# Linear attention and a low-rank mixer on one core: attention of the last batch four slots sooner, one more block pair by half products, second addends added by DMA

## The chip, the core and the metric

The kernel runs on one core of a Trainium2 chip. A core has five engines with their own instruction queues, each worked in program order: TensorE (PE, matrix products into PSUM, with its weight loads shown as PEld), VectorE (DVE), ScalarE (ACT), GpSimd (POOL) and SyncE (SP, here a queue that only issues DMAs). The metric is the device time of one execution in microseconds, as the median of several runs; lower is better.

## The reference

Eight batches, eight heads, 576 positions, head dimension 64. The first part is a linear attention whose features are a rectified input times a cosine and a sine of the position; the second is a low-rank mixing over positions followed by a two-layer network over channels with a residual:

```python
q_p = phi(q); k_p = phi(k)                      # relu(x)*cos, relu(x)*sin -> 128 features
kv  = einsum('bhsf,bhsd->bhfd', k_p, v)
x   = einsum('bhsf,bhfd->bhsd', q_p, kv) / (einsum('bhsf,bhf->bhs', q_p, sum_s k_p) + 1e-6)
x   = heads side by side                        # (8, 576, 512)
u   = x + (x^T @ U @ V)^T                       # rank 32, over positions
out = u + relu(u @ w_ch1) @ w_ch2               # 512 -> 2048 -> 512
```

All inputs and the output are fp32; the kernel computes its products in bf16 with fp32 sums.

## The kernel before

**Tiling.** A batch has 576 positions: four blocks of 128 (the "main" part) and 64 more. The 64 of two batches share one tile of 128, the "tail" of a batch pair. A batch's hidden layer is 2048 wide, 16 blocks of 128, each a unit `g1(b, j)`: four products of 128x128 weights with 512 columns of the transposed input `uT`, and one ScalarE eviction with the maximum into `hid`.

**Half products.** Where it pays in columns, the kernel uses a scheme with seven products in place of eight (sums and differences of quarter matrices, as Winograd's form of Strassen). For the second layer, `half_part(b, n, k, form)` computes output blocks n and n+2 of a batch together by seven steps of eight matmuls with 256 columns; `ORDER["with g"]` is the order of the products, (1, 2, 6, 5, 7, 3, 4). Their addends end in output tiles `o` (block n) and `o2` (block n+2) of the pool tag `o_sb`, a ring of eight buffers: products 1, 6 give first addends of `o`, products 2 and 3 the second ones; 5 and 4 first addends of `o2`, 7 a second one. For batches in `LENT = (5, 6)` the first addends are plain copies by ScalarE, and the input `u` is added by an accumulating DMA from GpSimd in `half_store`, before the block is stored. The sums of `hid` that the scheme needs are `hid_sum` (four for each half of a batch, on VectorE).

For the first layer, `g1_cross(b, p, i)` and `g1_join` do hidden blocks p and p+8 of a batch together ("pair p") by seven products of two matmuls with 256 columns: X and Y in one PSUM bank, Z in another (`CROSS`). ScalarE copies X or Z aside (P1, U2, P5), VectorE adds (C11, C22, C12), ScalarE and VectorE take the maximum. The helpers `opened` (products 1, 2), `sixth`, `fifth`, `third` (product 7) and `closed` (products 3, 4) put these in order. This needs sums of weights, `w1_sum(i, half)` (half 0 serves pairs 0 to 3, half 1 pairs 4 to 7), and of the transposed input, `uT_sum`. The weight sums lie in the buffers in which batch 7's queries and keys were loaded. Batch 7 has all its eight pairs done so, batch 6 its pairs 4 to 7.

**Order.** The order of the work is written out by hand. `slots` is a list of steps on TensorE; `todo` gives for a slot index the work beside it, issued right after the slot's own. From slot 88 the second layer of one batch alternates with the first layer of the next: slots 188 to 219 hold batch 6's first layer (`units`, odd slots from 191) beside batch 5's second (`beside_g`, even slots from 190); from slot 220 batch 7's first layer runs beside batch 6's second, and at the end batch 7's second layer runs alone.

`attention_plan(b)` places a batch's attention relative to a slot `w`, the first number of `PLAN[b]`: for batch 7, query features from w-24 (`q_prep`), key features and value casts from w-14 (`k_prep`, `v_prep`), three DMA transposes of the query features on SyncE (`qtr_dma`) at w-12, w-10, w-8, the two key-value products (`kv_unit`) at w and w+2, five `x_unit` from w+3 in steps of two, the rank-32 product (`A_unit`) at w+14, its expansion (`u_mm`) at w+16 and w+19 with four VectorE adds (`u_add`), two DMA transposes to `uT` (`utr_dma`) at w+17 and w+21, and the tail's part (`u_tail`) at w+23 and w+25. The `x_unit`s share one pair of banks (tag X). Batch 7's inputs are loaded by the plan of batch 6, at slots 149 and 153; batch 6's own `uT` transposes stand at slots 174 and 178.

Of the kernel before, what the change touches and what calls it, by code (L numbers as in the profile page):

```python
# [13 lines left out]
ALU = mybir.AluOpType  # L14
# [3 lines left out]
def kernel(  # L18
# [11 lines left out]
    nc = tc.nc  # L30

    B = 8
# [94 lines left out]
    def cast(eng, o, i):  # L127
        if eng is nc.scalar:
            nc.scalar.activation(out=o, in_=i, func=AF.Copy, bias=0.0, scale=1.0)  # L129
        else:  # L130
            eng.tensor_copy(out=o, in_=i)  # L131


    V_, A_, G_ = nc.vector, nc.scalar, nc.gpsimd
# [34 lines left out]
    def load_v0():  # L169
# [13 lines left out]
        out=iota[:, 0:4], pattern=[[2, 4]], base=0, channel_multiplier=9,  # L183
        allow_small_or_imprecise_dtypes=True,
    )
    for lo in (0, TS):
        nc.gpsimd.iota(
            out=iota[lo : lo + TS, 4:5], pattern=[[1, 1]], base=8, channel_multiplier=18,
# [380 lines left out]
    def g1_main(b, j, half=False):  # L569
        if b not in hid:  # L570
            hid[b] = pool.tile([P, NJ, 512], BF16, tag="hid", bufs=2, name="hid")
        g_ps = g_open.pop((b, j), None)
        d0 = 0 if g_ps is None else 2
        if g_ps is None:
            g_ps = ps.tile([P, 512], FP32, tag="g", bufs=3, name="g_ps")
        if half:
            g_open[b, j] = g_ps
        for d in range(d0, 2 if half else 4):
            nc.tensor.matmul(  # L579
                out=g_ps.rearrange("p (c t) -> p c t", c=4),  # L580
                lhsT=w1_bf[:, d, j * P : j * P + P],
                rhs=uT[b][:, d, :, :],
                start=(d == 0),
                stop=(d == 3),
            )
        if half:
            return
        nc.scalar.activation(  # L588
            out=hid[b][:, j, :], in_=g_ps, func=AF.Relu, bias=0.0, scale=1.0
        )  # L590
# [55 lines left out]
        }[i]()  # L646
        diff(uT_s[b, i], x, y)

    CROSS = [("g0", "g1"), ("g2", "T")]

    def g1_cross(b, p, i):

        if (b, p) not in cross:
            if b not in hid:
                hid[b] = pool.tile([P, NJ, 512], BF16, tag="hid", bufs=2, name="hid")
            of_x, of_z = CROSS[p % 2] if b == B - 1 else (("g0", "g1")[p % 2], "T")
            xy = psum.tile([P, 512], FP32, tag=of_x, bufs=1, name="c_ps")
            cross[b, p] = {"X": xy[:, 0:256], "Y": xy[:, 256:512], "of_z": of_z}  # L660
        w = cross[b, p]
        if i == 5:
            z = psum.tile([P, 512], FP32, tag=w["of_z"], bufs=1, name="c_ps")
            w["Z"] = z[:, 0:256]
        cs = slice(p * P, p * P + P)
        to, lhs, rhs, first = {
            1: lambda: ("X", W1[0], uT_quarter(b, 0, 0), True),
            2: lambda: ("Y", W1[1], uT_quarter(b, 1, 0), False),
            3: lambda: ("Z", w1_s[4], uT_quarter(b, 1, 1), False),
            4: lambda: ("X", W1[3], uT_s[b, 4], False),  # L670
            5: lambda: ("Z", w1_s[1], uT_s[b, 1], True),
            6: lambda: ("X", w1_s[2], uT_s[b, 2], False),
            7: lambda: ("X", w1_s[3], uT_s[b, 3], False),
        }[i]()
        for d in range(2):
            nc.tensor.matmul(  # L676
                out=w[to].rearrange("p (c t) -> p c t", c=2), lhsT=lhs[:, d, cs],
                rhs=rhs[:, d], start=(first and d == 0), stop=(d == 1),
                skip_group_check=not first,
            )  # L680
# [164 lines left out]
    def by_n(t):  # L845
        return t.rearrange("p (j n) -> p j n", n=P)
# [17 lines left out]
    def half_part(b, n, k, form):  # L864


        c2 = n + 2
        i = ORDER[form][k]
        if k == 0:
            halves[b, n] = {  # L870
                "o": [
                    pool.tile([P, DM], FP32, tag="o_sb", bufs=8, name="o_sb") for _ in range(2)
                ]
            }
            if form == "alone":
                halves[b, n]["s"] = pool.tile([P, DM], FP32, tag="o_sb", bufs=8, name="s_sb")
        w = halves[b, n]
        s1, s2 = hid_s.get((b, n, 1)), hid_s.get((b, n, 2))
        to, lhs, rhs = {
            1: ("X", h_of(b, 0, n), W2[0]),  # L880
            2: ("Y", h_of(b, 1, n), W2[2]),
            3: ("Z", h_of(b, 1, n), W2[3]),
            4: ("X" if form == "with g" else "Q", h_of(b, 1, c2), w2_s[3]),
            5: ("Z", s1, w2_s[0]),
            6: ("X", s2, w2_s[1]),
            7: ("X", h_of(b, 0, c2), w2_s[2]),
        }[i]
        at = BANKS[form].get(i)
        if at is not None:
            w[to] = bank(at)  # L890
        acc = w[to][:, 0:256]
        for j in range(8):
            nc.tensor.matmul(  # L893
                out=acc, lhsT=lhs[:, j, :], rhs=rhs[:, j, :],
                start=(j == 0 and at is not None), stop=(j == 7),
                skip_group_check=at is None,
            )
        lo, hi = slice(0, 256), slice(256, 512)
        o, o2 = w["o"]
        u = [[u_of(b, c, g) for g in range(2)] for c in (n, c2)]  # L900

        def first(t, cs, c, g):
            add(V_, by_n(t[:, cs]), u[c][g], by_n(acc))

        def more(t, cs):
            add(V_, t[:, cs], t[:, cs], acc)

        if form == "alone":
            ss = w["s"]
            if i == 1:  # L910
                cast(A_, ss[:, lo], acc)
            elif i == 2:
                first(o, lo, 0, 0)
            elif i == 5:
                cast(A_, o2[:, hi], acc)
            elif i == 6:
                cast(A_, ss[:, hi], acc)
            elif i == 4:
                cast(A_, o2[:, lo], acc)
                add(G_, by_n(o2), by_n(o2), u_bf[b][:, :, c2, :])  # L920
            elif i == 3:
                first(o, hi, 0, 1)
                add(G_, o, o, ss)
            elif i == 7:
                o2v = o2.rearrange("p (g n) -> p g n", g=2)
                add(V_, o2v, o2v, acc.unsqueeze(1).to_broadcast([P, 2, 256]))
        elif i in (1, 6, 5, 4):
            t, cs, c, g = {1: (o, lo, 0, 0), 6: (o, hi, 0, 1), 5: (o2, hi, 1, 1), 4: (o2, lo, 1, 0)}[i]
            if b in LENT:
                cast(A_, t[:, cs], acc)  # L930
            else:
                first(t, cs, c, g)
        elif i == 2:
            more(o, lo)
        elif i == 3:
            more(o, hi)
        else:
            if form == "last":
                more(o2, lo)
            more(o2, hi)  # L940
        if i == 2:
            behind.append(lambda: hid_sum(b, n, 4))
        if k == 6:
            turn[0] += 1

    def half_store(b, n, i):
        eng = nc.gpsimd if b < B - 2 else nc.sync
        c = n + 2 * i
        if b in LENT:
            o = halves[b, n]["o"][i]  # L950
            nc.gpsimd.dma_start(out=by_n(o), in_=u_bf[b][:, :, c, :], accum_op=ALU.add)  # L951
        eng.dma_start(  # L952
            out=out[b].rearrange("(m k) n -> m k n", k=9)[:, c : c + 6 : 5, :],
            in_=halves[b, n]["o"][i],
        )
# [28 lines left out]
    def spare(at):  # L984
# [11 lines left out]
        4: (100, (-20, 1, V_, V_), (-13, 2, A_, V_), -12, (-9, -4, -4)),  # L996
        5: (127, (-24, 2, A_, A_), (-14, 2, A_, V_), (-14, -8, -5), (-8, -4, -4)),
        6: (157, (-23, 2, A_, A_), (-14, 2, A_, V_), (-14, -8, -6), (-8, -4, -4)),
        7: (189, (-24, 2, A_, A_), (-14, 2, A_, V_), (-12, -10, -8), ()),
    }  # L1000

    def attention_plan(b):
# [351 lines left out]
    def g1(b, j):  # L1354
        return lambda: g1_main(b, j)
# [41 lines left out]
    def opened(b, p):  # L1397
        g1_cross(b, p, 1)
        g1_cross(b, p, 2)
        g1_join(b, p, "P1")  # L1400
        g1_join(b, p, "C11")
# [20 lines left out]
    def crossed(*steps):  # L1422
        def go():
            for f, b, p in steps:
                f(b, p)

        return go
# [11 lines left out]
    sums(b6 - 1, 0, (at, at + 1, at + 3))  # L1439
    sums(b6 - 1, 1, (at + 14, at + 16, at + 19))  # L1440
    for i, half, sl in (
        (1, 1, -8), (2, 1, -6), (3, 1, -4), (1, 0, -3), (4, 1, -2), (3, 0, -1), (2, 0, 11), (4, 0, 23),
    ):
        put(at + sl, lambda i=i, half=half: w1_sum(i, half))
    for i in range(4):
        put(at + (1, 2, 3, 7)[i], lambda i=i: uT_sum(b6, i + 1))
    units = [g1(b6, j) for p in range(3) for j in (p, p + 8)] + [g1(b6, 3)]
    units.append(lambda: [opened(b6, 4), g1_main(b6, 11)])
    units.append(crossed((sixth, b6, 4)))
    for p in range(5, 8):  # L1450
        units.append(crossed((opened, b6, p), (fifth, b6, p - 1), (third, b6, p - 1)))
        units.append(crossed((closed, b6, p - 1), (sixth, b6, p)))
    units.append(crossed((fifth, b6, 7), (third, b6, 7)))
# [129 lines left out]
```

## Time and profile before

| | |
|---|---|
| time, median of 3 runs | 292.39 us (292.39 to 292.65) |
| the profiled execution | 293.94 us, its span 292.2 us |
| instructions in the span | 7317 |
| TensorE busy | 283.5 us (97%) |
| VectorE busy | 208.0 us (71%) |
| ScalarE busy | 169.6 us (58%) |
| GpSimd busy | 56.1 us (19%) |
| bytes moved by DMA | 56.19 MB |

A row of a timeline gives the start in us from the span's start, the length, the engine, the line of the kernel, the operation, "written<-read" tiles, the shape, a count where like neighbours are merged and, in brackets, the idle time before it with what ended it. Matmuls are pipelined, so their lengths overlap; what TensorE takes is read from start to start. "SPq" rows are SyncE issuing a DMA, not the transfer. A row of grouped instructions has after the first bar the busy time and the mean length of one in ns, after the second the idle time before and what ended it.

### The profile page before, as it was taken

The numbers are of one execution on the slowest core, as the hardware profiler recorded it, in microseconds if no ns is written. First come the engines' busy times: TensorE is split into PE (matmuls) and PEld (weight loads), VectorE is DVE, ScalarE is ACT, GpSimd is POOL, SyncE is SP. The second block draws the span as 40 slices with busy tenths as digits, with TensorE's granted clock in tenths as the row PEclk, the third lists the DMA queues.
The fourth block names the chain that finished last, engine by engine and source line by source line (L and its number), as shares of the span: only waits on it lengthen the run. The fifth ranks groups of instructions, "written<-read, shape, count | busy, mean of one in ns | idle before, by whom it ended". The sixth has DMA issues, their size and how long they took to land.

```text
span 292.2 us, 7317 instructions
## 1 busy us (share of the span) xinstructions
PE 283.5 (97%) x2910; PEld 194.2 (66%) x2944; DVE 208.0 (71%) x503; ACT 169.6 (58%) x353; POOL 56.1 (19%) x92
## 2 busy tenths in 40 slices
PE   8989999999999999999999999999999999999994
PEld 4675554446645545777757666766777889889883
DVE  5877765487876687838746695678968787775773
ACT  2955663077692867579735865397654556657210
POOL 6420500000020001410500321022101223303330
PEclk9999999999999999999999999999999999999999
DMA  6999999899997999999779929992900964436023
GB/s 227 297 255 251 278 170 185 180 349 210 319 239 116 285 266 221 237 307 313 138 182 259 315 57 247 213 365 59 240 15 7 124 130 87 86 96 139 8 97 123
DMA packets 95175, 56.19 MB, mean 192 GB/s; under 512 B 58692, under 2 KB 91844, under 8 KB 95140
## 3 DMA queue, kind: packets, MB, share of 16 engines
q1 hardware_dynamic: 84420, 43.94, 61.4%
q0 software_dynamic: 10528, 11.57, 19.7%
q8 instruction: 23, 0.38, 0.5%
q10 hardware_dynamic: 192, 0.20, 0.2%
q14 instruction: 12, 0.10, 0.1%
HBM read 36.86 MB, written 9.44 MB: 158 GB/s over the span
## 4 chain that ended last, share of the span: by engine, by line
PE 89%; DVE 4%; DMA 3%; issue 1%; SPq 1%; ACT 0%; DVEq 0%; ACTq 0%
PE g_ps L579 29%; PE h_ps L893 26%; PE o_ps L761 10%; PE c_ps L676 5%; PE gt_ps L721 5%; PE kv_ps L347 3%; DMA vst<-in_v_dram 3%; PE x_ps L422 3%; PE a_ps L445 1%; PE h_ps L761 1%; PE g_ps L596 1%; DVE u_bf L483 1%; PE va_ps L475 1%; PE t_ps L365 1%; DVE hid L611 1%
## 5 line engine op out<-in xcount | busy, mean ns | idle before, releaser
L579 PE MATMUL g_ps<-uT,w_bf 128*128 128x512 bf16 x378 | 95.4, 379 | 1.2
L588 ACT ACTIVATE hid<-g_ps 128x512 bf16<-128x512 f32 x104 | 61.2, 600 | 57.1 <-PE g_ps L579 56.3
L579 PEld LDWEIGHTS <-w_bf 128*128 128x128 bf16 x402 | 37.5, 98 | 34.5 <-DMA w_bf<-in_moe_w_ch_dram 0.4
L893 PEld LDWEIGHTS <-hid 128*128 128x128 bf16 x480 | 45.5, 98 | 9.5
L893 PE MATMUL h_ps<-w_bf,hid 128*128 128x256 bf16 x288 | 37.1, 273 | 0.0
L761 PE MATMUL o_ps<-w_bf,hid 128*128 128x512 bf16 x122 | 29.4, 379 | 0.4 <-issue 0.2
L893 PE MATMUL h_ps<-w_s,S 128*128 128x256 bf16 x208 | 26.5, 273 | 0.0
L131 POOL CAST v_ext<-vst 128x512 bf16<-128x512 f32 (+1 forms) x23 | 15.2, 687 | 58.6 <-issue 25.4
L893 PE MATMUL h_ps<-w_s,hid 128*128 128x256 bf16 x192 | 24.9, 273 | 0.0
L849 DVE TENSOR_TENSOR o_sb<-o_sb,h_ps 128x256 f32<-128x256 f32 (+1 forms) x36 | 15.5, 432 | 12.6 <-PE h_ps L893 10.1
L893 PEld LDWEIGHTS <-S 128*128 128x128 bf16 x208 | 20.1, 98 | 4.4
L952 POOL DMA_DIRECT2D out_dram<-o_sb x16 | 9.9, 619 | 65.2 <-DVE o_sb L849 50.6
L483 DVE TENSOR_TENSOR u_bf<-x_bf,va_ps 128x512 bf16<-128x512 bf16 x27 | 17.6, 680 | 6.5 <-PE va_ps L475 2.8
L849 DVE TENSOR_TENSOR o_sb<-u_bf,h_ps 128x256 f32<-128x256 bf16 x28 | 11.7, 416 | 13.2 <-PE h_ps L893 13.1
L611 DVE TENSOR_TENSOR hid<-kept,c_ps 128x256 bf16<-128x256 f32 x36 | 14.7, 417 | 8.3 <-ACT kept L129 4.6
L761 PEld LDWEIGHTS <-hid 128*128 128x128 bf16 x128 | 11.5, 98 | 12.2
L129 ACT ACTIVATE kept<-c_ps 128x256 f32<-128x256 f32 x36 | 12.6, 384 | 7.3 <-PE c_ps L676 7.2
L951 POOL DMA_DIRECT2D o_sb<-u_bf x8 | 10.4, 1302 | 31.2 <-DVE rec L413 15.6
L721 PE MATMUL gt_ps<-uT_tl,w_bf 128*128 128x128 bf16 x256 | 16.2, 219 | 0.0
L432 DVE TENSOR_TENSOR x_bf<-x_ps,rec 128x512 bf16<-128x512 f32 x22 | 15.2, 692 | 0.8
L721 PEld LDWEIGHTS <-w_bf 128*128 128x128 bf16 x256 | 15.1, 98 | 0.7
L306 ACT ACTIVATE k_p<-kst,cosw 128x512 bf16<-128x512 f32 x20 | 14.2, 713 | 0.1
(189 smaller groups left out, 455.0 us busy)
## 6 DMA issues: line engine op xcount, KB each, us to landing
qst<-in_q_dram SPq DMA_DIRECT2D x14, 512.0 KB, 5.9
kst<-in_k_dram SPq DMA_DIRECT2D x14, 512.0 KB, 6.7
vst<-in_v_dram SPq DMA_DIRECT2D x12, 512.0 KB, 6.7
out_dram<-o_sb POOLq DMA_DIRECT2D x19, 256.0 KB, 4.1
out_dram<-o_sb SPq DMA_DIRECT2D x16, 256.0 KB, 2.5
w_bf<-in_moe_w_ch_dram POOLq DMA_DIRECT2D x7, 512.0 KB, 14.6
o_sb<-u_bf POOLq DMA_DIRECT2D x8, 256.0 KB, 3.7
qst<-in_q_dram SPq DMA_DIRECT2D x2, 640.0 KB, 13.6
```

The source lines that it names most:

```text
L131: eng.tensor_copy(out=o, in_=i)
L306: nc.scalar.activation(out=o, in_=i, func=AF.Relu, bias=0.0, scale=w)
L432: nc.vector.tensor_tensor(out=x_of(b, c, rows).rearrange("p (g i d) -> p g i d", g=2, d=D), in0=view[:, :, :, 0:D], in1=rec[rows].unsqueez ...
L483: nc.vector.tensor_tensor(out=u_bf[b][:, j, :, :], in0=x_bf[b][:, :, ns], in1=va[b][j].rearrange("p (c n) -> p c n", c=4), op=ALU.add,)
L579: nc.tensor.matmul(out=g_ps.rearrange("p (c t) -> p c t", c=4), lhsT=w1_bf[:, d, j * P : j * P + P], rhs=uT[b][:, d, :, :], start=(d == 0) ...
L588: nc.scalar.activation(out=hid[b][:, j, :], in_=g_ps, func=AF.Relu, bias=0.0, scale=1.0)
L611: V_.tensor_tensor(out=o, in0=x, in1=y, op=op)
L676: nc.tensor.matmul(out=w[to].rearrange("p (c t) -> p c t", c=2), lhsT=lhs[:, d, cs], rhs=rhs[:, d], start=(first and d == 0), stop=(d == 1 ...
L721: nc.tensor.matmul(out=g_ps[:, jj, :], lhsT=w1_bf[:, d, j * P : j * P + P], rhs=uT_tl[pr][:, d, :], start=(d == 0), stop=(d == 3),)
L761: nc.tensor.matmul(out=o[:, cols], lhsT=lhs[:, j, c * P : c * P + P], rhs=w2_bf[:, j, cols], start=(j == 0), stop=(j == NJ - 1),)
L849: eng.tensor_tensor(out=o, in0=x, in1=y, op=ALU.add)
L893: nc.tensor.matmul(out=acc, lhsT=lhs[:, j, :], rhs=rhs[:, j, :], start=(j == 0 and at is not None), stop=(j == 7), skip_group_check=at is ...
```

## The change

Four things change. The attention of batch 7 is placed from slot 185, not 189; everything in its plan moves with it, while its loads stay at slots 149 and 153. Pair 3 of batch 6 is done by half products like pairs 4 to 7; since pairs then begin with an odd one, the banks of `CROSS` swap. The eight weight sums are placed anew. And for batches 5 and 6, products 2 and 3 are no longer added on VectorE: ScalarE copies them to a scratch tile of the same ring of eight, and one more accumulating DMA of GpSimd adds the scratch to `o`.

```diff
-    CROSS = [("g0", "g1"), ("g2", "T")]
+    CROSS = [("g1", "g0"), ("g2", "T")]
...
-            of_x, of_z = CROSS[p % 2] if b == B - 1 else (("g0", "g1")[p % 2], "T")
+            of_x, of_z = CROSS[p % 2] if b == B - 1 else (("g1", "g0")[p % 2], "T")
...
-            if form == "alone":
+            if form == "alone" or b in LENT:
                 halves[b, n]["s"] = pool.tile([P, DM], FP32, tag="o_sb", bufs=8, name="s_sb")
...
+        elif b in LENT and i in (2, 3):
+            cast(A_, w["s"][:, lo if i == 2 else hi], acc)
         elif i == 2:
             more(o, lo)
         elif i == 3:
...
             nc.gpsimd.dma_start(out=by_n(o), in_=u_bf[b][:, :, c, :], accum_op=ALU.add)
+            if i == 0:
+                nc.gpsimd.dma_start(out=o, in_=halves[b, n]["s"], accum_op=ALU.add)
...
-        7: (189, (-24, 2, A_, A_), (-14, 2, A_, V_), (-12, -10, -8), ()),
+        7: (185, (-24, 2, A_, A_), (-14, 2, A_, V_), (-12, -10, -8), ()),
...
     for i, half, sl in (
-        (1, 1, -8), (2, 1, -6), (3, 1, -4), (1, 0, -3), (4, 1, -2), (3, 0, -1), (2, 0, 11), (4, 0, 23),
+        (1, 0, -8), (2, 0, -6), (3, 0, -4), (1, 1, -3), (2, 1, -1), (4, 0, 7), (3, 1, 9), (4, 1, 13),
     ):
         put(at + sl, lambda i=i, half=half: w1_sum(i, half))      # at is slot 188
...
-    units = [g1(b6, j) for p in range(3) for j in (p, p + 8)] + [g1(b6, 3)]
-    units.append(lambda: [opened(b6, 4), g1_main(b6, 11)])
-    units.append(crossed((sixth, b6, 4)))
-    for p in range(5, 8):
+    units = [g1(b6, j) for p in range(2) for j in (p, p + 8)] + [g1(b6, 2)]
+    units.append(lambda: [opened(b6, 3), g1_main(b6, 10)])
+    units.append(crossed((sixth, b6, 3)))
+    for p in range(4, 8):
         units.append(crossed((opened, b6, p), (fifth, b6, p - 1), (third, b6, p - 1)))
         units.append(crossed((closed, b6, p - 1), (sixth, b6, p)))
```

## The prediction

> **What bounds the kernel now.** I read the page first, then the chain of waits in order of time, then the timelines of TensorE (PE), VectorE (DVE), SyncE's queue and GpSimd (POOL) between 175 and 292 us. A "slot" is one entry of the kernel's hand-written list; step times below are slots placed on the timeline by their matmuls.
>
> ```profile
> span 292.2 us, 7317 instructions
> PE 283.5 (97%) x2910; PEld 194.2 (66%) x2944; DVE 208.0 (71%) x503; ACT 169.6 (58%) x353; POOL 56.1 (19%) x92
> ...
> PE 89%; DVE 4%; DMA 3%; issue 1%; SPq 1%; ACT 0%; DVEq 0%; ACTq 0%
> ```
>
> TensorE is the bound, and it issues almost without a break. A saving therefore has two sources only: fewer columns to stream, or a place where TensorE stands still. In the stretch that the change touches I find one such place, from TensorE's timeline:
>
> ```profile
> 227.38 0.60 PE L676 MATMUL c_ps<-uT,w_bf 128*128 128x256 bf16 x4
> ...
> 237.11 0.39 PE L676 MATMUL c_ps<-uT,w_s 128*128 128x256 bf16 x2
> 237.63 0.38 PE L676 MATMUL c_ps<-uT_s,w_bf 128*128 128x256 bf16 x2
> ```
>
> Two matmuls of 256 columns take 0.22 us from start to start (eight take 0.87, below), so the fourth product of pair 6 could have begun at 237.33 and began at 237.63: 0.3 us lost. It writes into a bank that C22 of that pair still reads. VectorE's timeline shows why that read was late:
>
> ```profile
> 228.44 0.75 DVE L611 TENSOR_TENSOR hid<-kept,c_ps 128x256 bf16<-128x256 f32 x2 [1.73 <-ACT kept L129]
> 229.11 0.68 DVE L483 TENSOR_TENSOR u_bf<-x_bf,va_ps 128x512 bf16<-128x512 bf16 x1
> 229.77 0.42 DVE L849 TENSOR_TENSOR o_sb<-o_sb,h_ps 128x256 f32<-128x256 f32 x1
> 230.11 0.68 DVE L483 TENSOR_TENSOR u_bf<-x_bf,va_ps 128x512 bf16<-128x512 bf16 x1
> 230.71 0.68 DVE L835 TENSOR_TENSOR hid<-hid,S 128x1024 bf16<-128x1024 bf16 x1
> 231.31 0.42 DVE L611 TENSOR_TENSOR hid<-kept,c_ps 128x256 bf16<-128x256 f32 x1
> 231.97 0.68 DVE L835 TENSOR_TENSOR hid<-hid 128x1024 bf16<-128x1024 bf16 x1
> ...
> 236.84 0.74 DVE L611 TENSOR_TENSOR hid<-kept,c_ps 128x256 bf16<-128x256 f32 x2
> ```
>
> VectorE waits 1.73 us for pair 5's first product, then works without a gap: its queue, in program order, is what TensorE waits for at 237.33. C22 of pair 6 is the second half of the row at 236.84. The starts give the prices of a full queue: an attention add (L483) 0.60 to 0.66, a hidden-sum (L835) 0.60, an output addend (L849) 0.34, C11 with C22 0.67, C12 with its maximum 0.66. Everywhere else from here to the end TensorE's starts follow each other at the streaming rate, so a gain is at most this 0.3 us and what the half products save.
>
> **The half products.** Pair 3 of batch 6 leaves eight matmuls of 512 columns and takes fourteen of 256.
>
> ```profile
> 209.84 1.89 PE L579 MATMUL g_ps<-uT,w_bf 128*128 128x512 bf16 x7
> 211.57 0.29 PE L347 MATMUL kv_ps<-v_ext,k_p 128*128 128x65 bf16 x4
> ...
> 212.18 1.04 PE L893 MATMUL h_ps<-w_bf,hid 128*128 128x256 bf16 x8
> 213.05 1.03 PE L579 MATMUL g_ps<-uT,w_bf 128*128 128x512 bf16 x4
> ...
> 217.38 0.42 PE L422 MATMUL x_ps<-kv,q_pT 128*128 128x65 bf16 x8
> 217.64 1.02 PE L579 MATMUL g_ps<-uT,w_bf 128*128 128x512 bf16 x4
> ```
>
> Eight of 512 take 1.73 us (209.84 to 211.57), eight of 256 take 0.87 (212.18 to 213.05), so fourteen take 1.52: TensorE has 0.20 us less. The pair also moves work: two ScalarE evictions of 512 columns go, five ScalarE passes and three VectorE adds and a maximum (0.67 + 0.66, 1.3 us of VectorE) come. The eight weight sums are only reordered; two that stood at slots 184 and 186 now stand at 197 and 201, and those of 199 and 211 go to 182 and 195. The bank names swapped at L649 and L658 keep the old alternation, since the pairs now start one earlier: nothing.
>
> **The second addends.**
>
> ```profile
> L129 ACT ACTIVATE o_sb<-h_ps 128x256 f32<-128x256 f32 x20 | 7.6, 382 | 8.6 <-PE h_ps L893 8.3
> ```
>
> Eight VectorE adds (two products, two halves of a batch, two batches) leave, 8 x 0.34 = 2.7 us of VectorE's queue, and eight ScalarE copies of 0.382 come, 3.1 us. ScalarE is 58% busy and a copy holds its bank no longer than an add of 0.42 (229.77) did, so on ScalarE I put nothing; if that cover went, each copy would hold a bank 0.38 us. GpSimd gets four accumulating transfers more:
>
> ```profile
> 224.33 1.32 POOL L951 DMA_DIRECT2D o_sb<-u_bf  x1 [15.59 <-DVE rec L413]
> ...
> 228.26 0.63 POOL L952 DMA_DIRECT2D out_dram<-o_sb  x1 [2.62 <-DMA o_sb<-u_bf]
> ...
> 234.68 0.63 POOL L952 DMA_DIRECT2D out_dram<-o_sb  x1 [4.48 <-DMA o_sb<-u_bf]
> ...
> 251.72 1.29 POOL L951 DMA_DIRECT2D o_sb<-u_bf  x1 [3.45 <-DVE o_sb L849]
> ...
> 263.06 1.27 POOL L951 DMA_DIRECT2D o_sb<-u_bf  x1 [8.57 <-DVE o_sb L849]
> ...
> 274.69 1.16 POOL L849 TENSOR_TENSOR o_sb<-o_sb,u_bf 128x512 f32<-128x512 f32 x1 [8.64 <-ACT o_sb L129]
> ```
>
> GpSimd waits for each accumulate to land before the next access: 3.9 us in the first case (224.33 to 228.26), 5.8 in the second (its issue follows the store at 228.26 + 0.63). The new one moves as many bytes of output, so its bounds are 3.9 and 5.8; I take 3.9, since its rows are as long as a store's and no transposes run beside most of them. From 224.5 batch 5 then holds GpSimd for 2 x (3 x 3.9 + 2 x 0.63) = 26 us, until 250.5, and batch 6's first output is ready at 251.72. Batch 6's second half starts at 263.06, its first store can go at 263.06 + 7.8 = 270.9 and its last accumulate is issued by 272.2, before batch 7's add at 274.69. So what is queued behind these waits (the stores, then batch 7's adds) has room. The output ring has eight buffers, and each half of batches 5 and 6 now takes three: the closest reuse is the scratch of batch 7's second half, written after the add at 274.69, on the buffer whose store went at 270.9. Nothing, at 3.9.
> The Trainium skill, page "DMA: Bandwidth & Descriptors", section "Rules for kernel authors", says that an accumulate next to another access of the same bytes must wait for the earlier transfer's semaphore. The wait of 2.62 us above agrees. The same page's fit for a GpSimd transfer ("Anatomy of one DMA — SWDGE (gpsimd) path") makes 256 KB an estimated 2.6 us, by which batch 5 would end about 5 us sooner and the sum would not change.
>
> **The attention of batch 7.** All of it moves four slots, with its loads left where they are. The query features now start at slot 161; their second step, behind the eviction of slot 163, writes a buffer that batch 6's query transposes still read:
>
> ```profile
> 179.36 5.93 SPq L391 DMA_TRANSPOSE q_pT<-q_p x1
> ...
> 199.79 1.25 SPq L521 DMA_TRANSPOSE uT<-u_bf x1
> ...
> 205.19 4.90 SPq L391 DMA_TRANSPOSE q_pT<-q_p x2
> ...
> L391 SPq DMA_TRANSPOSE q_pT<-q_p x12: 1476/2878/5952, 66.0 to 206.8; - x12
> ...
> DMA to landing us min/median/max: 3.7/6.4/10.0
> ...
> DMA to landing us min/median/max: 2.7/2.7/4.5
> ...
> 187.19 0.60 ACT L588 ACTIVATE hid<-g_ps 128x512 bf16<-128x512 f32 x1 [1.40 <-PE g_ps L579]
> ```
>
> (The two landing rows are those of L391 and of L521.) ScalarE gets there at 187.19 + 0.60 = 187.8 and may wait to 179.36 + 10.0 = 189.4; the evictions behind it are late by up to 1.6 us, but each bank is written again only two evictions, some 4 us, later: nothing. The key features and value casts move into time that VectorE and GpSimd have.
> The two kv units move from slots 189 and 191 to 185 and 187. Each takes 0.61 (211.57 to 212.18), so slot 188 starts at 209.84 + 1.22 = 211.06.
> The five x units move from 192-200 to 188-196, into the same slots as three hidden-sums and three sums of the transposed input. VectorE's prices:
>
> ```profile
> 207.82 1.29 DVE L611 TENSOR_TENSOR w_s<-w_bf 128x1024 bf16<-128x1024 bf16 x2
> ...
> 212.02 0.42 DVE L611 TENSOR_TENSOR uT_s<-uT,uT_s 128x512 bf16<-128x512 bf16 x1
> 212.36 0.68 DVE L835 TENSOR_TENSOR hid<-hid 128x1024 bf16<-128x1024 bf16 x1
> ...
> 215.65 0.42 DVE L849 TENSOR_TENSOR o_sb<-o_sb,h_ps 128x256 f32<-128x256 f32 x1 [2.27 <-ACT kv L129]
> ...
> 217.99 0.17 DVE L412 TENSOR_SCALAR rec<-x_ps 128x8 f32<-128x8 f32 x1
> ...
> 219.03 0.42 DVE L611 TENSOR_TENSOR uT_s<-uT,uT_s 128x512 bf16<-128x512 bf16 x1
> ```
>
> A weight sum takes 0.60, a sum of uT 0.34 (its full 0.42 before one that needs it), an x unit 1.04. The idle 2.27 us, ended at 215.65 by an addend that now leaves VectorE, are what the x units fill. By hand: three weight sums from 207.82 and the first hidden-sum are done by 210.3; the first x unit's matmuls end near 212.3, its VectorE part near 213.5; hidden-sum and two uT sums (0.60 + 0.42 + 0.34) bring the second x unit to 214.9 and its last read of the shared bank, 1.1 later, to 216.0. TensorE wants that bank for the third at 211.06 + 5 x 0.87 + 2 x 0.26 = 215.9 and has it some 0.1 after that read: it waits 0.2 us (0 to 0.5 with the error of eight steps).
> Now the stretch of the 0.3 us. Before, from slot 205 (227.38) to the fourth product of slot 215, TensorE's list is five groups of a pair, five half products, the attention's 16 and 8 small matmuls; after, slots 201 to 211 hold exactly that list for pairs one lower. VectorE starts each list on time (idle before C11). Its list between has, after against before, two hidden-sums more (those of slots 202 and 204 fall between the attention adds), two addends fewer, and one weight sum in both: 2 x 0.60 - 2 x 0.34 = +0.52. The wait of 0.3 becomes 0.8, spread over fifth and fourth products of pairs 3 to 5. Bounds: 0, since ScalarE's and VectorE's order may fit better than by this count, to 1.2. Past slot 212 VectorE has four attention adds, a weight sum and an addend less than it had, and the old wait at 237.33 is not met again.
> SyncE's queue changes order: the second half of batch 6's uT transposes (slot 178) came ahead of batch 7's two q_pT transposes and now comes behind them. They take SyncE 4.9 us from 201.1, so it is issued at 206.0 and lands 2.7 later, 208.7, for a need at slot 188's third matmul, 211.06 + 0.43 = 211.5: nothing, if it lands as before.
> **Sum:** -0.20 + 0.2 + (0.8 - 0.3) = +0.5 us. The profiled execution took 293.94 us, 1.7 around its span and 1.55 over the median; the sum applies to the median, 292.39: 292.9 us, 0.17% more.
>
> **Rivals.** *VectorE keeps up* (25%): its queue falls by 2.7 - 1.3 = 1.4 us over the two batches and the attention adds move out of the old jam. Then no wait is left: 292.39 - 0.20 - 0.3 = 291.9. Against it: the list of the jam, counted above, grows by 0.52.
>
> *The uT half lands late* (17%): a q_pT transpose issued at 201.1 + 1.6 = 202.7 lands 6.4 (median) to 10.0 us later, 209.1 to 212.7; if the uT half moves only behind it, TensorE stands before slot 188 from the point where that landing passes 211.5, by 1.2 us at 212.7. The 0.2 at the x bank then goes: 292.39 - 0.20 + 0.5 + 1.2 = 293.9, slower. Against it: the median lands 2.4 us inside the need. The Trainium skill (same page, "Queues, rings and completion order") says that each engine consumes descriptors in ring order and that SyncE owns one ring on each; by that rule the half does go behind, and whether TensorE waits is left to the landing.
> *Accumulates of 5.8 us* (4%): batch 5 then holds GpSimd for 2 x (3 x 5.8 + 1.3) = 37 us, to 262, batch 6's halves follow at 262 and 275, and the store at 275 + 11.6 = 286 lets ScalarE write a buffer that it wants soon after 274.69: up to 10 us, 302. Against it: the first of the two waits shown is 3.9. That the change does not do what it says I hold at 4%, at 292.4.
>
> **How the numbers follow.** Forecast 50%, at 292.9 with 292.5 to 293.3 its own range. The range for 8 in 10 goes from the first rival's 291.9 to the second's 293.9. A difference of 0.2% (0.58 us) is about what a measurement of this kernel can tell from no change. Even the full gain of 0.5 us stays inside it, so faster is 6%; within takes somewhat over half of the forecast (27), most of the first rival (19) and the case of no effect (4), 50%; slower takes the rest of the forecast and the second and third rivals, 44%.
>
> **What would show it.** Right: TensorE gaps of 0.1 to 0.5 us before fifth and fourth products of pairs 3 to 5 (near 216 and 228 to 235 us), none at slot 215, VectorE without idle time between. Wrong: no gaps there (first rival), one gap before the first g matmuls of batch 6 with uT as its releaser (second), or ScalarE waiting on an output buffer's DMA (third). A change over 2 us either way would mean a wait that I have not seen.

## The result, and the profile after

The changed kernel is slower: 293.71 us in the median of 22 runs, against 293.0 us for the kernel before in the runs beside them; the ratio is 1.0032, with a 95% interval from 1.0018 to 1.0045 (0.5 to 1.3 us). Forecast was 1.0017, called no change. (The 292.39 us of three runs lies low among the 22, which go from 292.19 to 294.06.)

The page of the profile after, its first lines and the engines of the chain that ended last:

```profile
span 292.5 us, 7392 instructions
PE 285.5 (98%) x2950; PEld 194.2 (66%) x2950; DVE 207.6 (71%) x499; ACT 171.9 (59%) x364; POOL 61.5 (21%) x96
...
PE 83%; DMA 5%; DVE 4%; ACT 3%; SPq 2%; issue 1%; DVEq 0%; ACTq 0%
```

The page hides the answer: every busy share has hardly moved, and the two spans differ by 0.3 us only. Spans of single executions also hold what happens in the first 20 us (last section), so I read a stretch that both kernels share: from batch 6's rank-32 product (slot 171, before anything that is changed on TensorE) to the second group of tail products at slot 221 (after all of it on TensorE). From TensorE's timeline, before and then after, with TensorE's last group at the end:

```profile
195.06 0.24 PE L445 MATMUL a_ps<-x_tl,U_bf 128*32 128x128 bf16 x4
...
241.14 1.06 PE L721 MATMUL gt_ps<-uT_tl,w_bf 128*128 128x128 bf16 x16
...
287.12 1.04 PE L893 MATMUL h_ps<-w_bf,hid_tl 128*128 128x256 bf16 x8
```

```profile
194.66 0.24 PE L445 MATMUL a_ps<-x_tl,U_bf 128*32 128x128 bf16 x4
...
241.52 1.06 PE L721 MATMUL gt_ps<-uT_tl,w_bf 128*128 128x128 bf16 x16
...
287.47 1.04 PE L893 MATMUL h_ps<-w_bf,hid_tl 128*128 128x256 bf16 x8
```

46.08 us before, 46.86 after: +0.78 in this stretch, although it holds 0.20 us less to stream. Behind it, where batch 6's addends fall, TensorE takes 45.98 us to its last group before and 45.95 after, and 45.95 to 45.98 in every experiment, so nothing is lost there. TensorE's timeline after shows the places:

```profile
214.63 1.04 PE L893 MATMUL h_ps<-w_bf,hid 128*128 128x256 bf16 x8
215.84 0.43 PE L422 MATMUL x_ps<-kv,q_pT 128*128 128x65 bf16 x8 [0.17 <-DVE x_bf L432]
...
226.75 1.04 PE L893 MATMUL h_ps<-w_bf,hid 128*128 128x256 bf16 x8
228.17 0.39 PE L475 MATMUL va_ps<-A_sb,V_bf 32*128 32x128 bf16 x4 [0.39 <-DVE u_bf L483]
...
234.12 0.39 PE L676 MATMUL c_ps<-uT,w_s 128*128 128x256 bf16 x2
234.73 0.38 PE L676 MATMUL c_ps<-uT_s,w_bf 128*128 128x256 bf16 x2 [0.22 <-DVE hid L611]
```

Eight matmuls of 256 columns stream in 0.87 us. So the third x unit, due at 215.50, starts 0.34 late; the second part of `u_mm`, due at 227.62 and some 0.1 later in the kernel before as well (231.19 in place of 231.09), is 0.46 later still; the fourth product of pair 5, due at 234.34, 0.39 late. (The bracket counts from the modelled end of a matmul and shows less.) With two gaps of 0.05 to 0.06 that is 1.3 us; less the old wait of 0.3 and the columns' 0.20 it makes +0.8, the whole stretch. All three releasers are VectorE. Its timeline there:

```profile
211.97 0.17 DVE L412 TENSOR_SCALAR rec<-x_ps 64x8 f32<-64x8 f32 x1 [2.02 <-PE x_ps L422]
...
213.13 0.69 DVE L835 TENSOR_TENSOR S<-S,hid 128x1024 bf16<-128x1024 bf16 x1
213.75 0.42 DVE L611 TENSOR_TENSOR uT_s<-uT 128x512 bf16<-128x512 bf16 x1
214.19 0.42 DVE L611 TENSOR_TENSOR uT_s<-uT,uT_s 128x512 bf16<-128x512 bf16 x1
214.65 0.17 DVE L412 TENSOR_SCALAR rec<-x_ps 128x8 f32<-128x8 f32 x1
...
215.09 0.69 DVE L432 TENSOR_TENSOR x_bf<-x_ps,rec 128x512 bf16<-128x512 f32 x1
...
224.96 0.75 DVE L611 TENSOR_TENSOR hid<-kept,c_ps 128x256 bf16<-128x256 f32 x2 [2.02 <-ACT kept L129]
225.63 0.68 DVE L611 TENSOR_TENSOR w_s<-w_bf,w_s 128x1024 bf16<-128x1024 bf16 x1
226.23 0.68 DVE L483 TENSOR_TENSOR u_bf<-x_bf,va_ps 128x512 bf16<-128x512 bf16 x1
226.83 0.68 DVE L835 TENSOR_TENSOR S<-hid 128x1024 bf16<-128x1024 bf16 x1
227.43 0.68 DVE L483 TENSOR_TENSOR u_bf<-x_bf,va_ps 128x512 bf16<-128x512 bf16 x1
...
229.62 0.75 DVE L611 TENSOR_TENSOR hid<-kept,c_ps 128x256 bf16<-128x256 f32 x2 [0.25 <-ACT kept L129]
...
233.93 0.75 DVE L611 TENSOR_TENSOR hid<-kept,c_ps 128x256 bf16<-128x256 f32 x2
```

VectorE is not short of time: it idles 2.02 us twice, with the head of its queue waiting for a product (the second time for ScalarE's copy of one), while hidden-sums, the first time sums of uT too, stand behind; that these were ready is shown below, where they run in that time. Then they run ahead of what TensorE needs: the x unit at 215.09, whose read frees the shared bank, and the second attention add at 227.43, which frees the same bank for `u_mm`.

### The profile page after: what moved, and what is told of

Read it like the earlier page. It is cut to its first block, busy times and chain, and to the rows that moved or that the text cites. A ratio compares the mean times of both kernels' runs of the same rounds, so it can differ in the third digit from the quotient of the medians.

```text
span 292.5 us, 7392 instructions
## 1 busy us (share of the span) xinstructions
PE 285.5 (98%) x2950; PEld 194.2 (66%) x2950; DVE 207.6 (71%) x499; ACT 171.9 (59%) x364; POOL 61.5 (21%) x96
## 4 chain that ended last, share of the span: by engine, by line
PE 83%; DMA 5%; DVE 4%; ACT 3%; SPq 2%; issue 1%; DVEq 0%; ACTq 0%
PE g_ps L579 27%; PE h_ps L893 24%; PE o_ps L761 10%; PE c_ps L676 6%; PE gt_ps L721 5%; DMA q_pT<-q_p 4%; PE kv_ps L347 2%; PE x_ps L422 2%; DMA qst<-in_q_dram 2%; PE a_ps L445 1%; PE g_ps L596 1%; PE va_ps L475 1%; SPq L391 1%; DVE u_bf L483 1%; PE t_ps L365 1%
## 5 line engine op out<-in xcount | busy, mean ns | idle before, releaser
L588 ACT ACTIVATE hid<-g_ps 128x512 bf16<-128x512 f32 x102 | 59.7, 597 | 54.1 <-PE g_ps L579 53.7
L579 PEld LDWEIGHTS <-w_bf 128*128 128x128 bf16 x394 | 36.7, 97 | 34.4 <-issue 0.8
L761 PE MATMUL o_ps<-w_bf,hid 128*128 128x512 bf16 x128 | 30.1, 379 | 0.0
L131 POOL CAST v_ext<-vst 128x512 bf16<-128x512 f32 (+1 forms) x23 | 16.3, 735 | 62.8 <-DMA vst<-in_v_dram 33.0
L611 DVE TENSOR_TENSOR hid<-kept,c_ps 128x256 bf16<-128x256 f32 x39 | 16.0, 418 | 11.7 <-ACT kept L129 6.0
L849 DVE TENSOR_TENSOR o_sb<-o_sb,h_ps 128x256 f32<-128x256 f32 (+1 forms) x28 | 12.1, 434 | 8.3 <-PE h_ps L893 8.0
L129 ACT ACTIVATE kept<-c_ps 128x256 f32<-128x256 f32 x39 | 13.6, 384 | 6.1 <-PE c_ps L676 6.1
L721 PEld LDWEIGHTS <-w_bf 128*128 128x128 bf16 x256 | 15.0, 98 | 0.5
L953 POOL DMA_DIRECT2D o_sb<-u_bf x8 | 11.0, 1370 | 14.7 <-ACT o_sb L129 13.4
```

The costliest lines, as they stand in the source:

```text
L579: nc.tensor.matmul(out=g_ps.rearrange("p (c t) -> p c t", c=4), lhsT=w1_bf[:, d, j * P : j * P + P], rhs=uT[b][:, d, :, :], start=(d == 0) ...
L588: nc.scalar.activation(out=hid[b][:, j, :], in_=g_ps, func=AF.Relu, bias=0.0, scale=1.0)
L611: V_.tensor_tensor(out=o, in0=x, in1=y, op=op)
L721: nc.tensor.matmul(out=g_ps[:, jj, :], lhsT=w1_bf[:, d, j * P : j * P + P], rhs=uT_tl[pr][:, d, :], start=(d == 0), stop=(d == 3),)
L761: nc.tensor.matmul(out=o[:, cols], lhsT=lhs[:, j, c * P : c * P + P], rhs=w2_bf[:, j, cols], start=(j == 0), stop=(j == NJ - 1),)
L849: eng.tensor_tensor(out=o, in0=x, in1=y, op=ALU.add)
```

## The experiments

Theory one: VectorE's order makes TensorE wait. Theory two: the accumulating transfers cost the time. Theory three: the joins of pair 3 cost more than its columns save. Besides the timed ratio against the kernel before (its 95% interval in brackets) I give "the stretch", the time between the two rows shown above, taken from each run's own timeline.

**The parts alone.** Four kernels, made of the change's own hunks.

```diff
-        7: (189, (-24, 2, A_, A_), (-14, 2, A_, V_), (-12, -10, -8), ()),
+        7: (185, (-24, 2, A_, A_), (-14, 2, A_, V_), (-12, -10, -8), ()),   # attention alone
```

> The kernel before with the attention of batch 7 four slots sooner, nothing else. Theory one (VectorE's queue is late where the x units now meet the hidden sums, and TensorE waits for banks): waits of 0.4 to 0.8 us in all at the shared x bank in slots 190 to 196, the wait of 0.3 before the fourth product at slot 215 gone; +0.2 to +0.5 us. Theory two (the added accumulating transfers cost the time): no difference but the old wait gone, -0.3 to 0. Theory three (the joins of pair 3 cost more than its columns save): -0.3 to 0.

1.0036 (1.0019 to 1.0053); the stretch 47.23 us, +1.15. The attention's place alone costs more than the whole change. Two gaps at the x bank (0.34 and 0.40 us by their starts), and the old wait did not go: it stands at slot 211 with a second one ahead of it.

```profile
231.68 0.61 PE L676 MATMUL c_ps<-uT,w_bf 128*128 128x256 bf16 x4
232.42 0.60 PE L676 MATMUL c_ps<-uT_s,w_s 128*128 128x256 bf16 x4
...
234.61 0.38 PE L676 MATMUL c_ps<-uT_s,w_bf 128*128 128x256 bf16 x2 [0.22 <-DVE hid L611]
```

Four matmuls from 231.68 end their streaming at 232.12, so the next starts 0.30 late. The mechanism of theory one, at more than twice the price expected.

```diff
...
+    units = [g1(b6, j) for p in range(2) for j in (p, p + 8)] + [g1(b6, 2)]   # pair alone
+    units.append(lambda: [opened(b6, 3), g1_main(b6, 10)])
...
```

> The kernel before with pair 3 of batch 6 by half products (with the weight sums and banks placed for it), nothing else. Theory one: 0.20 us of columns less and the weight sum of slot 211 out of the jam, so the wait before slot 215's fourth product goes: -0.3 to -0.5 us. Theory two: -0.2. Theory three: +0.5 to +0.9, with TensorE gaps at the products of pairs 3 to 5.

0.9994 (0.9978 to 1.001); the stretch 46.06, -0.02. The gain that theory one expected is missing: the old wait is gone, but a gap of 0.37 at the x bank and one of 0.08 at a fourth product have come (below). Theory three is out: alone the pair costs nothing in sum.

```diff
...
+        elif b in LENT and i in (2, 3):
+            cast(A_, w["s"][:, lo if i == 2 else hi], acc)      # addends alone
...
+                nc.gpsimd.dma_start(out=o, in_=halves[b, n]["s"], accum_op=ALU.add)
```

> The kernel before with the second addends of batches 5 and 6 copied by ScalarE and added by DMA, nothing else. Theory one: VectorE loses 0.34 us ahead of slot 215, the old wait of 0.3 goes: -0.3 us, no new gap on TensorE. Theory two: +0.5 to +0.9, ScalarE or TensorE waiting for an output buffer or a bank. Theory three: -0.3 to 0.

0.9995 (0.9978 to 1.0012); the stretch 46.08, the same as before. Theory two is out, and so is a piece of theory one: the old wait stayed, though an addend had left VectorE ahead of it. TensorE's and VectorE's timelines of this kernel:

```profile
236.63 0.39 PE L676 MATMUL c_ps<-uT,w_s 128*128 128x256 bf16 x2
237.15 0.38 PE L676 MATMUL c_ps<-uT_s,w_bf 128*128 128x256 bf16 x2
```

```profile
232.16 0.75 DVE L611 TENSOR_TENSOR hid<-kept,c_ps 128x256 bf16<-128x256 f32 x2 [0.39 <-ACT kept L129]
...
236.35 0.74 DVE L611 TENSOR_TENSOR hid<-kept,c_ps 128x256 bf16<-128x256 f32 x2
```

The 0.34 us saved became 0.39 us of waiting for pair 6's first copy at 232.16, where VectorE starts afresh. In the kernel before it had all but caught up at the same place, since the hidden-sum ahead (231.97, price 0.60) leaves some 0.07 us:

```profile
232.64 0.75 DVE L611 TENSOR_TENSOR hid<-kept,c_ps 128x256 bf16<-128x256 f32 x2
```

Only what VectorE does after its last such start makes TensorE wait: from there to the row with the C22 that TensorE needs it takes 4.20 us before (232.64 to 236.84) and 4.19 here (232.16 to 236.35), and TensorE waits 0.30 us in both.

```diff
-        7: (185, (-24, 2, A_, A_), (-14, 2, A_, V_), (-12, -10, -8), ()),
+        7: (189, (-24, 2, A_, A_), (-14, 2, A_, V_), (-12, -10, -8), ()),   # the change, less the attention
```

> The changed kernel with the attention of batch 7 back at slot 189. Theory one: no VectorE wait left in slots 188 to 219: -0.5 us against before, some 1.3 less than the changed kernel. Theory two: +0.4 or more. Theory three: +0.3 or more.

0.999 (0.9974 to 1.0007); the stretch 46.06, 0.8 us less than the changed kernel but no gain over the one before, where theory one expected 0.5: the pair's gaps of 0.37 and 0.08 are here too.

**VectorE's order.** On the changed kernel, only VectorE's instructions moved.

```diff
-    sums(b6 - 1, 1, (at + 14, at + 16, at + 19))
+    sums(b6 - 1, 1, (at + 10, at + 11, at + 22))          # hidden-sums moved
```

> The changed kernel with only the three hidden-sums of batch 5's second half moved: slots 202 and 204 to 198 and 199, where VectorE sat idle for 2.0 us, and 207 to 210. Theory one (VectorE's order, not its load or any transfer, is what TensorE waits for): the gap before the second part of u_mm (0.46 us) and that before the fourth product at slot 211 (0.38) go, the two at the x bank (0.39) stay: -0.8 us against the changed kernel, about +0.1 against the one before. A theory of transfers or of ScalarE being full: no difference.

1.0005 (0.9981 to 1.0028); the stretch 46.04, -0.82 against the changed kernel. As expected to 0.02 us: the gaps before `u_mm` and at slot 211 are gone, those at the x bank stay.

```diff
-    sums(b6 - 1, 0, (at, at + 1, at + 3))
+    sums(b6 - 1, 0, (at, at, at + 3))
...
-        put(at + (1, 2, 3, 7)[i], lambda i=i: uT_sum(b6, i + 1))
+        put(at + (-1, -1, 3, 7)[i], lambda i=i: uT_sum(b6, i + 1))
```

> The changed kernel with one hidden-sum and two uT sums moved ahead of the first x unit (from slots 189, 189 and 190 to 188, 187 and 187), into the other idle time of 2.0 us. Theory one: the two gaps at the x bank (0.39 us) go, the later ones stay or grow by little, since VectorE waits for pair 4 in between: -0.4 us against the changed kernel, +0.5 against the one before. Other theories: no difference.

1.0013 (0.9997 to 1.0028); the stretch 46.47, -0.39: the x bank's gaps are gone, the others as in the changed kernel (0.46 and 0.38).

> Both moves together. Theory one: no wait of TensorE left in slots 188 to 219: -1.2 us against the changed kernel and, with the 0.20 us of columns and the old wait of 0.3 gone, -0.5 against the one before. Other theories: no difference from the changed kernel.

0.9988 (0.9969 to 1.0007), and a second time:

> The kernel with both moves once more, to narrow its interval. Theory one: -0.45 us against the one before by TensorE's stretch from slot 171 to slot 221, a ratio near 0.9985.

0.9997 (0.9975 to 1.0019); the stretch 45.64 both times, -1.22 against the changed kernel and -0.44 against the one before. TensorE's rows of the first:

```profile
193.64 0.24 PE L445 MATMUL a_ps<-x_tl,U_bf 128*32 128x128 bf16 x4
...
239.28 1.06 PE L721 MATMUL gt_ps<-uT_tl,w_bf 128*128 128x128 bf16 x16
```

The two moves add up (0.82 + 0.39 = 1.21), with no transfer, copy or product changed. So the loss was VectorE's order. That this kernel beats the one before is shown for the stretch, not by the timed ratio, whose two intervals both hold 1.

**What the addends are worth.** The changed kernel without them, plain and with both moves:

```diff
-        elif b in LENT and i in (2, 3):
-            cast(A_, w["s"][:, lo if i == 2 else hi], acc)
...
```

> The changed kernel without its second addends: VectorE adds products 2 and 3 of batches 5 and 6 again, and GpSimd's four extra transfers are gone. Theory one: four adds of 0.34 us come back into VectorE's list in slots 192 to 214, so the gaps at the x bank grow from 0.39 us to some 0.7 and the later ones stay or grow: +0.3 to +0.7 us against the changed kernel. If the transfers or ScalarE's copies cost anything: faster than the changed kernel.

> The same kernel with the two moves of hidden-sums and uT sums. Theory one: the returned adds still meet the x units, gaps of 0.3 to 0.6 us at the x bank, none at u_mm and slot 211: -0.2 to +0.2 us against the one before, some 0.4 slower than the kernel with the moves and with the second addends. If the second addends are worth nothing: equal to it, -0.45 against the one before.

1.0055 (1.0039 to 1.0071) with a stretch of 47.54, and 1.0009 (0.9996 to 1.0022) with 46.19. The addends are worth 0.68 us in the changed kernel and 0.55 with both moves. With the attention at slot 189 they are worth nothing, neither in the kernel before (46.08 twice) nor beside the pair (46.06 twice): VectorE's adds cost only where they meet the earlier attention. The places were expected in part: with both moves the gap at the x bank is 0.22 us, less than the 0.3 expected, and another of 0.32 stands before the fifth product of pair 5 (slot 209), where none was expected.

**Why pair 3 alone gains nothing.** Three weight sums were moved from the neighbourhood of the x units into idle time of VectorE (with the attention at slot 189):

```diff
-        ... (2, 1, -1), (4, 0, 7), (3, 1, 9), (4, 1, 13),
+        ... (2, 1, -1), (4, 0, 3), (3, 1, 3), (4, 1, 3),
```

> The attention back at slot 189, pair 3 and the addends as in the changed kernel, and the three weight sums of slots 195, 197 and 201 at slot 191, where VectorE sat idle for 2.95 us. Theory one: the gaps of 0.37 and 0.08 that were left go: -0.45 us against the same kernel without that move, -0.5 against the one before. If the attention's place had a worth of its own, this would be slower than the kernel with both moves; by theory one they are equal.

1.0009 (0.9993 to 1.0026), the stretch 46.05: a miss, the gap is unmoved. TensorE's timeline of this kernel says why, then VectorE's:

```profile
220.83 0.42 PE L422 MATMUL x_ps<-kv,q_pT 128*128 128x65 bf16 x8
221.09 0.38 PE L676 MATMUL c_ps<-uT_s,w_s 128*128 128x256 bf16 x2
221.30 1.04 PE L893 MATMUL h_ps<-w_bf,hid 128*128 128x256 bf16 x8
222.54 0.43 PE L422 MATMUL x_ps<-kv,q_pT 128*128 128x65 bf16 x8 [0.21 <-DVE x_bf L432]
```

```profile
221.03 0.42 DVE L849 TENSOR_TENSOR o_sb<-o_sb,h_ps 128x256 f32<-128x256 f32 x1 [0.72 <-PE h_ps L893]
...
221.80 0.69 DVE L432 TENSOR_TENSOR x_bf<-x_ps,rec 128x512 bf16<-128x512 f32 x1
```

VectorE is idle here until 221.03, so it is not full. Slot 199, between the x units of slots 198 and 200, holds one product of 0.22 us since pair 3 is done by halves, where a unit of 0.86 stood. So the last x unit is due 1.34 us after the one before it (220.83 to 222.17), and VectorE holds the bank until 222.49, 1.66 us after that one began. The addend at 221.03 is at most a small part of this: the second x unit of this kernel, which nothing delays, holds the bank 1.59 us (216.40 to 217.99). So the last x unit was moved to where a longer slot separates it:

```diff
-                put((3 if b == B - 1 else 4) + 2 * n, x_unit, c, "X", 1)
+                put((3 if b == B - 1 else 4) + 2 * n + (b == B - 1 and n == 4), x_unit, c, "X", 1)
```

> The kernel with the attention at slot 189, pair 3, the addends and the weight sums at slot 191, and now the last x unit one slot later (201, not 200). Reason to be tested: the gap of 0.37 us that stayed there comes from slot 199, which pair 3 shortens to one product of 0.22 us, so that two x units follow each other faster than VectorE can empty the bank. If so, the gap goes and the stretch from slot 171 to slot 221 takes 45.6 to 45.7 us, as with the attention four slots sooner and both moves. If the gap comes from VectorE's load, it moves with the x unit and the stretch stays at 46.05.

0.9969 (0.995 to 0.9988), 292.29 us in the median against 292.98. This beats the kernel before, and with it the changed one. Its rows:

```profile
193.41 0.24 PE L445 MATMUL a_ps<-x_tl,U_bf 128*32 128x128 bf16 x4
...
239.13 1.06 PE L721 MATMUL gt_ps<-uT_tl,w_bf 128*128 128x128 bf16 x16
```

45.72 us, at the top of what was expected, with the attention where it was: moving it four slots is one way around the short slot 199, but needs both moves of VectorE's work to come out as well. The stretch is 0.36 us shorter than before; the timed ratio says 0.35 to 1.5 us, and the runs do not show that the gain is larger than the stretch's. Whether the three weight sums have to be at slot 191 for it was not tried.

## Why the prediction was right or wrong

**Right.** TensorE's columns: with all waits gone the stretch falls by 0.44, against 0.20 of columns and 0.3 of the old wait. The x bank is where the x units meet hidden-sums and sums of uT, and the third x unit is the one that waits. No gap is left at slot 215. ScalarE waits for batch 6's query transposes, and nothing comes of it:

```profile
188.65 0.72 ACT L306 ACTIVATE q_p<-qst,cosw 128x512 bf16<-128x512 f32 x1 [1.26 <-DMA q_pT<-q_p]
```

SyncE's order changed as said, and the second half of batch 6's uT goes out behind both q_pT transposes; TensorE did not wait for it at slot 188:

```profile
200.90 3.85 SPq L391 DMA_TRANSPOSE q_pT<-q_p  x2
204.85 1.26 SPq L521 DMA_TRANSPOSE uT<-u_bf  x1
```

The pair took SyncE 3.85 us, not 4.9, and the half went out at 204.85, not 206.0. The ring order that the Trainium skill states ("DMA: Bandwidth & Descriptors", "Queues, rings and completion order") decided nothing here.
The accumulates: GpSimd's wait was priced at 3.9 us each.

```profile
240.22 0.88 POOL L955 DMA_DIRECT2D o_sb<-s_sb  x1 [3.34 <-ACT kept L129]
243.79 0.64 POOL L956 DMA_DIRECT2D out_dram<-o_sb  x1 [2.69 <-DMA o_sb<-s_sb]
```

From the scratch's accumulate to the store that follows it are 3.6 us, nearer to the row's 3.9 than to the 2.6 of the Trainium skill's fit (same page, "Anatomy of one DMA — SWDGE (gpsimd) path"). By that fit batch 5's six accumulates would end 7.8 us sooner, not the 5 of the prediction, which changes nothing. ScalarE is shown waiting for one of the scratch's accumulates, 0.28 us at 243.49, the third rival's sign in small; TensorE lost nothing by it (45.95 us from slot 221 on, above).

**Wrong.** The failed step is the sum's two waits, in size, and with them the call of "no change": +0.5 us was forecast, and the stretch shows +0.78. The x bank was put at 0.2 us and took 0.40: the count had the third x unit 0.2 late, the trace has it 0.34 late and the fourth 0.06. From the end of the first x unit to the last read of the second the count has 0.60 + 0.42 + 0.34 + 1.1 = 2.46 us and the rows have 2.65 (213.13 to 215.78); most of the difference is the second sum of uT, which holds VectorE 0.46 us (214.19 to 214.65) and not 0.34. (The prediction speaks of three sums of uT among the x units; there are four, the last behind the third x unit.)

The jam was put at 0.8 in place of 0.3 and took 0.90. That this is near is partly luck. I let VectorE's lateness add up along the whole list and fall on fifth and fourth products. It does not add up: VectorE waits for ScalarE's copy at C11s on the way and starts even (some 0.07 us idle before 232.64 in the kernel before, where I read no gap; 0.25 before 229.62 after). Counted from the last such start the list grew from 4.20 to 4.31 us (229.62 to 233.93), and the wait before the fourth product from 0.30 to 0.39: on fourth and fifth products together the jam costs 0.44 us, not 0.8. The other half, 0.46, falls where I had named no bank: `u_mm`'s second part reuses the pair of banks of the x units, and waits for the second attention add, which a hidden-sum now precedes. A weight sum stands ahead of it as well (225.63); I counted one "in both", but before it came behind the attention adds, at the end of the list (235.32). Alone it is not the cause: with only the hidden-sums moved it stays there and the wait is gone. The kernel with addends alone, where the list grew shorter and the wait stayed, refutes the whole list as the measure; the kernel with hidden-sums moved, -0.82, shows what stands in its place. Of the signs that I named, a late fourth product of pair 5 and a quiet slot 215 were met; VectorE without idle time was not.

The call failed by the threshold too: I took 0.2% for what can be told from no change, and the measured interval reaches 0.13 to 0.14% to either side, so that even the forecast 0.17% would have stood clear of it.

Of the rivals, VectorE keeping up is refuted: it has the time (idle 2.02 us twice) and is still late. The late uT half did not occur, nor did long accumulates of the scratch, which landed 3.3 to 3.5 us after their issue. The range, 291.9 to 293.9, holds the measured median; on the base of 292.39 that the sum used, the measured ratio gives 293.3, the top of the forecast's own range.

## What to carry to other kernels

An engine with idle time can still be the one waited for: look at what stands ahead, in its queue, of the instruction that frees a bank, and put ready work into the idle stretch before a known wait rather than after it. Lateness doesn't carry past an instruction that has to wait for something else anyway, so count from the last such instruction. And when a unit becomes shorter, check what was spaced by its length: saving columns at slot 199 took away the time in which a bank was emptied.

## What the runs showed that was not expected

The three parts don't add. Alone they change the stretch by +1.15, -0.02 and 0.00 us; together by +0.78; attention and pair without the addends by +1.46. A part can be tested alone only for what it costs, not for what it is worth beside the others.

A single span is a poor witness for half a microsecond. In the profiled execution after, the first rank-32 product starts 1.65 us sooner than before (18.23 against 19.88):

```profile
19.88 0.23 PE L445 MATMUL a_ps<-x_tl,U_bf 128*32 128x128 bf16 x2
```

```profile
18.23 0.23 PE L445 MATMUL a_ps<-x_tl,U_bf 128*32 128x128 bf16 x2
...
148.18 0.59 PE L579 MATMUL g_ps<-uT,w_bf 128*128 128x512 bf16 x2 [0.47 <-DMA uT<-u_bf]
...
160.79 0.43 PE L422 MATMUL x_ps<-kv,q_pT 128*128 128x65 bf16 x8 [0.49 <-DMA q_pT<-q_p]
```

Further on, TensorE waited twice, 0.63 and 0.64 us by the starts, for transposes of batch 5, which the change does not touch; of the other thirteen profiles (the one before and the experiments') one shows the second of these waits, at 0.36 us, and none the first. By slot 171 only 0.40 us of the lead was left (194.66 against 195.06). The stretch from there to slot 221 came out equal to 0.01 us in the two runs of the same kernel, and so could tell what the spans could not.
